# Replacing the framework's scheduler by hand-made semaphores, a TensorE hardware loop and a turned MLP in a decode layer

## The chip, the cores and the metric

The kernel runs on one core of one Trainium2 chip. The metric is the device time of one launch in microseconds (us). All times here are medians of several runs, unless a text says "profiled run", which means the one execution that the hardware profiler recorded. The profiler's span, from the first to the last recorded instruction, is about 1.8 us shorter than the device time of the same run.

Engines are named as the profile names them: PE is TensorE (matmuls), PEld its weight loads, DVE VectorE, ACT ScalarE, POOL GpSimd, SP SyncE. A trailing "q" (SPq, PEq) means the sequencer of that engine. A DMA queue is a list of loads; 16 DMA engines share each bulk load, packet by packet (a tile of 8.39 MB is 128 packets of 64 KB), and the trace records one completion from each of the 16 shares.

## The reference, cut to what matters

It is one decode step of a transformer layer: two batch rows, one token each, 32 heads, and a key and value cache of 8192 positions per head.

```python
# x: (2,1,512)   k_cache, v_cache: (2,32,8192,128) bf16   wq: (512,4096)   wo: (4096,512)
def _A_ref(x, k_cache, v_cache, wq, wo):                 # attention
    q = (x @ wq) -> (2,32,1,128)
    scores = einsum("bhqd,bhkd->bhqk", q, k) * 128**-0.5
    p = softmax(scores)
    o = einsum("bhqk,bhkd->bhqd", p, v)
    return o.reshape(2,1,4096) @ wo
def _B_ref(x, W_gate, W_up, W_down):                     # F = 1376
    gate = x @ W_gate;  gate = gate * (gate > 0)
    return (gate * (x @ W_up)) @ W_down
h  = x + _A_ref(layernorm(x), ...)
h2 = h + _B_ref(layernorm(h), ...)
```

Keys and values are 268 MB of the 281.06 MB that must be read. There are no other large costs by nature: the kernel is a stream of loads with arithmetic beside it.

## The kernel before

Four heads form a "quad", 16 quads in all (8 per batch row). A quad's keys and its values are one tile of 128 x 32768 bf16 (8.39 MB) each. The kernel holds two key tiles and one value tile at a time. Per quad, VectorE multiplies the keys by the query, adds halves in a tree and reduces to scores; ScalarE takes the exponentials into `pm`; TensorE makes the 64 "V products" (128x512 each, spread over four column groups); VectorE sums the four "lanes" of the result; TensorE spreads them. All bulk loads are issued by SyncE into one DMA queue.

```python
# tile pools: kring bufs=2, vring bufs=1, ps_o bufs=2, ... ; the framework sets the semaphores
def lanes_of(o):                                               # 4 VectorE operations of 128x128
    nc.vector.tensor_scalar_mul(osb, o[:, 0:Dh], turn_of[:, 0:1])
    for t in range(1, TG):
        nc.vector.scalar_tensor_tensor(out=osb, in0=o[:, t*Dh:(t+1)*Dh], scalar=turn_of[:, t:t+1],
                                       in1=osb, op0=ALU.mult, op1=ALU.add)
# ... two quads of one row share one result tile o ("paired"), so lanes_of runs 10 times, not 16 ...
for n in range(N - 1):
    scores(n);  load_k(n + 2);  collect();  weighted_v(n);  load_v(n + 1)
# ... weights: output weights first, then the last V in four parts, then gate, up, down ...
nc.sync.dma_start(out=wol, in_=A_wo[LQ * G * Dh:, :].rearrange("(h d) n -> d h n", d=P))  # 1 KB pieces
# ... tail: weights of the MLP as the stationary operand, 88 matmuls of 2 columns ...
for c in range(KC):
    for fc in range(FC):
        nc.tensor.matmul(out=ps[0:w, fc, :], lhsT=lhsT, rhs=hd[:, c, :], ...)
```

The softmax here doesn't subtract the row's maximum and nothing guards it: scores larger than these inputs give would overflow.

Of the kernel before, what the change touches and what calls it, by code (L numbers as in the profile page):

```python
# [12 lines left out]
def _view(t, offset, dims):  # L13
    return bass.AP(tensor=t.tensor, offset=t.offset + offset, ap=[t.ap[0]] + list(dims))


@with_exitstack
def kernel(
# [33 lines left out]
    NM = 2  # L52
    Q = P // G
    ENG = mybir.EngineType

    assert Sq == 1 and Hkv == Hq and D == KC * P and Hq % (2 * G) == 0 and T % 32 == 0 and P == Dh

    consts = ctx.enter_context(tc.tile_pool(name="consts", bufs=1))
    misc = ctx.enter_context(tc.tile_pool(name="misc", bufs=1))
    kring = ctx.enter_context(tc.tile_pool(name="kring", bufs=2))  # L60
    vring = ctx.enter_context(tc.tile_pool(name="vring", bufs=1))
    spool = ctx.enter_context(tc.tile_pool(name="spool", bufs=1))
    opool = ctx.enter_context(tc.tile_pool(name="opool", bufs=1))
    ps_acc = ctx.enter_context(tc.tile_pool(name="ps_acc", bufs=1, space=bass.MemoryType.PSUM))
    ps_mm = ctx.enter_context(tc.tile_pool(name="ps_mm", bufs=2, space=bass.MemoryType.PSUM))
    ps_o = ctx.enter_context(tc.tile_pool(name="ps_o", bufs=2, space=bass.MemoryType.PSUM))
    ps_s = ctx.enter_context(tc.tile_pool(name="ps_s", bufs=1, space=bass.MemoryType.PSUM))

    mean_c = consts.tile([P, 1], f32)
    mean_f = _view(mean_c, 0, [[0, P]])  # L70
    zm = consts.tile([P, B, NQ - 1], f32)
    zl = consts.tile([P, B, G], f32)
    eps_t = consts.tile([P, 1], f32)
# [3 lines left out]
    pm = consts.tile([P, R + NG * W2], bf16)  # L77
    row_of = consts.tile([P, Q], f32)
    nc.vector.memset(eps_t, EPS)
    nc.vector.memset(mean_c, 1.0 / D)  # L80
    nc.vector.memset(zm, 0.0)
    nc.vector.memset(zl, 0.0)
    nc.vector.memset(row_of, 0.0)
    ident = consts.tile([P, P], bf16)
    masks.make_identity(nc, ident)
    zero = consts.tile([P, 1], bf16)
    nc.gpsimd.memset(zero, 0.0)
    nc.gpsimd.memset(pm, 0.0)

    SIZES = (4, 2, 1)  # L90
    FIRST = (0, 4, 6)
    turn_of = consts.tile([P, TG], f32)
    lane_of = consts.tile([P, 2, G], f32)
    head_blk = consts.tile([P, G], f32)
    half_blk = consts.tile([P, 2], f32)
    pick = {n: consts.tile([P, Q // n], f32, name=f"pick{n}") for n in SIZES}
    spread = {n: consts.tile([P, min(n, 2), G, Q // n], f32, name=f"spread{n}") for n in SIZES}
    same = {n: consts.tile([P, n, G, Q // n], f32, name=f"same{n}") for n in SIZES}

    def build_masks():  # L100
        def red(out, in_, axis=AXIS.X):
            nc.vector.tensor_reduce(out=out, in_=in_, axis=axis, op=ALU.add)

        red(turn_of, ident.rearrange("p (g t h) -> p t g h", t=TG, h=G), AXIS.XY)
        red(lane_of, ident.rearrange("p (g u t h) -> p u h g t", u=2, t=TG, h=G), AXIS.XY)
        red(head_blk, ident.rearrange("p (h m) -> p h m", h=G))
        red(half_blk, ident.rearrange("p (u m) -> p u m", u=2))
        red(row_of[:, 0:B], ident.rearrange("p (g q) -> p q g", q=Q)[:, 0:B, :])
        for n in SIZES:
            u = min(n, 2)  # L110
            red(pick[n], ident.rearrange("p (h m) -> p m h", m=Q // n))
            nc.vector.tensor_copy(spread[n], _view(lane_of, 0, [[G, u], [1, G], [0, Q // n]]))
            nc.vector.tensor_copy(same[n], _view(head_blk, 0, [[0, n], [1, G], [0, Q // n]]))

    ctx.enter_context(tc.manual_schedule(engines={ENG.PE, ENG.DVE, ENG.Activation, ENG.SP}))

    warm = consts.tile([1, 1], f32)
    nc.scalar.activation(out=warm, in_=eps_t[0:1, :], func=ACT.Sqrt)


    x_row = opool.tile([B, D], bf16, tag="row")
    nc.scalar.dma_start(out=x_row, in_=A_x.rearrange("b s d -> (b s) d"))
    RING = T * Dh
    wq_sb = vring.tile([P, RING], bf16, tag="v", name="wq_sb")[:, 0:KC * Hq * Dh].rearrange(
        "p (c n) -> p c n", c=KC)
    nc.sync.dma_start(out=wq_sb, in_=A_wq.rearrange("(p c) n -> p c n", p=P))

    def centred(hc, pfx):

        hs = misc.tile([P, B], f32, name=pfx + "hs")  # L130
        nc.vector.tensor_reduce(out=hs, in_=hc.rearrange("p c b -> p b c"), axis=AXIS.X, op=ALU.add)
        mu = ps_s.tile([P, B], f32, tag="st", name=pfx + "mu")
        nc.tensor.matmul(out=mu, lhsT=mean_f, rhs=hs, start=True, stop=True)
        return mu.unsqueeze(1).to_broadcast([P, KC, B])

    def variance(d, pfx):
        sq = misc.tile([P, KC, B], f32, name=pfx + "sq")
        nc.vector.tensor_tensor(out=sq, in0=d, in1=d, op=ALU.mult)
        ss = misc.tile([P, B], f32, name=pfx + "ss")
        nc.vector.tensor_reduce(out=ss, in_=sq.rearrange("p c b -> p b c"), axis=AXIS.X, op=ALU.add)  # L140
        var = ps_s.tile([P, B], f32, tag="st", name=pfx + "var")
        nc.tensor.matmul(out=var, lhsT=mean_f, rhs=ss, start=True, stop=True)
        return var


    x_ps = ps_s.tile([P, KC, B], f32, tag="st")
    x_v = x_row.rearrange("b (m c) -> b m c", c=KC)
    for c in range(KC):
        nc.tensor.matmul(out=x_ps[:, c, :], lhsT=x_v[:, :, c], rhs=ident[0:B, 0:B],  # L149
                         start=True, stop=True)  # L150
    xc = misc.tile([P, KC, B], f32)
    nc.vector.tensor_copy(xc, x_ps)  # L152
    xd = misc.tile([P, KC, B], f32)
    nc.vector.tensor_tensor(out=xd, in0=xc, in1=centred(xc, "ln1"), op=ALU.subtract)
    rstd = misc.tile([P, B], f32)
    nc.scalar.activation(out=rstd, in_=variance(xd, "ln1"), func=ACT.Sqrt, bias=eps_t, scale=1.0)
    nc.vector.reciprocal(out=rstd, in_=rstd)
    xn = misc.tile([P, KC, B], bf16)
    nc.vector.tensor_tensor(out=xn, in0=xd, in1=rstd.unsqueeze(1).to_broadcast([P, KC, B]),
                            op=ALU.mult)  # L160
    xnb = opool.tile([P, KC, B, Q], bf16, tag="row")
    nc.vector.tensor_copy(xnb, xn.unsqueeze(3).to_broadcast([P, KC, B, Q]))
    nc.scalar.activation(out=warm, in_=xn[0:1, 0, 0:1], func=ACT.Exp)
    build_masks()


    qrep = consts.tile([P, B, NQ, Dh], bf16)
    QP = 4
    wq_v = wq_sb.rearrange("p c (i h d) -> p c i h d", h=G, d=Dh)
    for g in range(0, NQ, QP):  # L170
        for h0 in range(0, G, 2):
            qps = ps_mm.tile([P, QP, Dh], f32, tag="mm", name="qps")
            for h in range(2):
                for c in range(KC):
                    nc.tensor.matmul(  # L175
                        out=qps[h * B * Q:(h + 1) * B * Q],
                        lhsT=xnb[:, c].rearrange("p b q -> p (b q)"),
                        rhs=wq_v[:, c, g:g + QP, h0 + h, :],
                        start=(c == 0), stop=(c == KC - 1),
                    )  # L180
            for b in range(B):
                for h in range(2):
                    src = qps[(h * B + b) * Q:(h * B + b + 1) * Q]
                    dst = qrep[(h0 + h) * Q:(h0 + h + 1) * Q, b, g:g + QP, :]
                    if h == 0:
                        nc.scalar.activation(out=dst, in_=src, func=ACT.Copy)  # L186
                    else:
                        nc.vector.tensor_copy(dst, src)  # L188


    seq = [(b, i) for b in range(B) for i in range(NQ)]
    N = len(seq)
    LQ = NQ - 1
    kts, vts = {}, {}

    def load_part(t, cache, n, lo, hi):
        b, i = seq[n]
        src = cache[b, G * i:G * i + G].rearrange("h s d -> (h s) d").rearrange(
            "(p t) d -> p t d", p=P)
        nc.sync.dma_start(out=t[:, lo:hi, :], in_=src[:, lo:hi, :])  # L200

    def load_k(n, cuts=(0, T)):
        kts[n] = kring.tile([P, T, Dh], bf16, tag="k", name="k")
        for lo, hi in zip(cuts[:-1], cuts[1:]):
            load_part(kts[n], A_k_cache, n, lo, hi)
# [83 lines left out]
    def collect():  # L289

        if not pair.get("done"):
            return
# [276 lines left out]
```

## Time and profile before

| What | Value | Where it is read |
|---|---|---|
| time | 661.36 us (661.24 to 661.72, 3 runs) | the runs |
| span of the profiled run | 659.4 us | head of the page |
| DMA queue busy | 98.9% of 16 engines | DMA queue section |
| VectorE busy | 609.6 us, 92% | busy section |
| TensorE busy | 119.5 us, 18% | busy section |
| last packet of the weights | 655.22 us | DMA records of the trace |
| output issued | 656.41 us | timeline of SyncE |
| end of the program | 659.43 us | last record |

The page of the kernel before. The first line gives, by engine, busy time, share and number of instructions; the DMA and GB/s lines are 40 slices of the span; the q lines give packets, MB and share of the 16 DMA engines; the lines with an L are groups of instructions (count, then busy time and mean ns of one, then idle time ahead of them and what ended it).

```profile
PE 119.5 (18%) x1341; PEld 58.6 (9%) x1341; DVE 609.6 (92%) x225; ACT 55.8 (8%) x142; POOL 2.5 (0%) x8
...
DMA  9999999999999999999999999999999999999996
GB/s 382 445 445 445 395 433 446 437 445 418 417 445 437 441 442 398 445 445 426 441 417 433 445 422 441 437 417 441 426 441 441 421 438 426 433 441 433 393 420 259
...
q1 hardware_dynamic: 7272, 281.06, 98.9%
q8 instruction: 10, 0.16, 0.1%
...
L257 PE MATMUL o<-v,pm 128*32 128x512 bf16 x1016 | 88.1, 522 | 395.8 <-DMA v<-in_A_v_cache_dram 395.8
...
L266 DVE TENSOR_SCALAR osb<-o,turn_of 128x128 f32<-128x128 f32 x10 | 3.4, 344 | 9.2 <-PE o L257 9.2
L268 DVE SCALAR_TENSOR_TENSOR osb<-o,turn_of,osb 128x128 f32<-128x128 f32 x30 | 10.5, 351 | 1.1
```

The DMA line is full from the first slice to the last but one. 281.06 MB in the 651 us between the head and the tail are 432 GB/s; the windows view gives 433 GB/s from 2 to 600 us (single slices above read up to 446). In the same trace a packet of 64 KB takes 2.42 us on its share (median of 3840 packets), which is 27.1 GB/s, and 16 such shares are 433 GB/s. So the queue moves what its packets allow, with no gap to close. TensorE waits 395.8 us for V tiles, so whatever is saved on TensorE is saved in idle time.

The slice below 400 GB/s near the end is one of the few things that can move. This is the windows view of the kernel before: the window, its length, busy time with the number of instructions for PE, PEld, DVE, ACT and POOL, TensorE clock, DMA share, GB/s.

```profile
610.00:625.00 15.00, 7.09 (x70) 3.30 (x70) 14.93 (x3) 0.00 (x0) 0.00 (x0) 0.61 0.95 386
```

Here the output weights of the last quad arrive in pieces of 1 KB (a packet of that size took 0.046 us in this trace, 22 GB/s on its share against the 27.1 of a 64 KB packet). The two last lines that matter are the load that starts VectorE's waits in the second half, in the chain of the kernel before (start, length, what), and the issue of the output, in its timeline of SyncE (start, length, what).

```profile
246.27 38.86 DMA k<-in_A_k_cache_dram
```

```profile
656.41 0.65 SPq L537 DMA_DIRECT2D out_dram<-y_row  x1
```

From 246 us on the chain steps through one key load after another, so until then VectorE and afterwards the queue is the one that ended last. VectorE's idle time between its first product of keys (24.49 us) and its last sums (631.86 us) adds up to 14.6 us.

### The profile page before, as it was taken

The page shows a single profiled execution, that of the slowest core. Times are in us where ns is not written, and L with a number is a line of the kernel's source. Part 1 is how long each engine was busy: PE and PEld are TensorE (multiplying, and loading weights), DVE is VectorE, ACT ScalarE, POOL GpSimd, SP SyncE. Part 2 cuts the span into 40 slices and gives each one's busy share as a digit, 9 for nine tenths or more (in the row PEclk, how much of TensorE's full clock was granted, in tenths as well). Part 3 has the DMA queues.
Part 4 walks back from the last instruction along what each step waited for, and adds up shares of the span by engine and source line. Part 5 has one row for each costly group of instructions (what it writes and reads, how often), then busy time and mean ns, then how long its engine had stood idle before and what let it go on. Part 6 is the DMA issues. An engine that isn't in the chain of part 4 may idle for free.

```text
span 659.4 us, 3234 instructions
## 1 busy us (share of the span) xinstructions
PE 119.5 (18%) x1341; PEld 58.6 (9%) x1341; DVE 609.6 (92%) x225; ACT 55.8 (8%) x142; POOL 2.5 (0%) x8
## 2 busy tenths in 40 slices
PE   2100302003030210303012130301202030020446
PEld 1000101001010100101001110100001010010225
DVE  2899999999999999999999999999999998999952
ACT  2201001010101001010101001010010101001020
POOL 1000000000000000000000000000000000000000
PEclk9555755757565575756557575555757555575656
DMA  9999999999999999999999999999999999999996
GB/s 382 445 445 445 395 433 446 437 445 418 417 445 437 441 442 398 445 445 426 441 417 433 445 422 441 437 417 441 426 441 441 421 438 426 433 441 433 393 420 259
DMA packets 7314, 281.26 MB, mean 427 GB/s; under 512 B 802, under 2 KB 1412, under 8 KB 2308
## 3 DMA queue, kind: packets, MB, share of 16 engines
q1 hardware_dynamic: 7272, 281.06, 98.9%
q8 instruction: 10, 0.16, 0.1%
q14 instruction: 4, 0.03, 0.0%
q10 hardware_dynamic: 28, 0.01, 0.0%
HBM read 281.06 MB, written 0.00 MB: 426 GB/s over the span
## 4 chain that ended last, share of the span: by engine, by line
DVE 62%; DMA 33%; PE 3%; issue 1%; ACT 0%; DVEq 0%
DMA k<-in_A_k_cache_dram 31%; DVE k L222 29%; DVE k L228 28%; DVE sc L231 4%; DMA wq_sb<-in_A_wq_dram 2%; DVE osb L268 1%; DVE qrep L188 1%; PE qps L175 1%; PE o L257 1%; PE ar_ps L452 0%; ACT qrep L186 0%; PE y_ps L466 0%; PE a_ps L459 0%; PE gate_ps L510 0%; PE up_ps L510 0%
## 5 line engine op out<-in xcount | busy, mean ns | idle before, releaser
L222 DVE TENSOR_TENSOR k<-k,qrep 128x32768 bf16<-128x32768 bf16 (+1 forms) x17 | 275.7, 16217 | 8.9 <-DMA k<-in_A_k_cache_dram 8.8
L228 DVE TENSOR_TENSOR k<-k 128x16384 bf16<-128x16384 bf16 (+3 forms) x68 | 266.8, 3923 | 2.3
L257 PE MATMUL o<-v,pm 128*32 128x512 bf16 x1016 | 88.1, 522 | 395.8 <-DMA v<-in_A_v_cache_dram 395.8
L234 ACT ACTIVATE pm<-sc 32x256 bf16<-32x256 f32 x64 | 47.2, 738 | 563.9 <-DVE sc L231 527.6
L257 PEld LDWEIGHTS <-pm 128*32 128x32 bf16 x1016 | 37.9, 127 | 444.8 <-issue 282.3
L231 DVE TENSOR_REDUCE sc<-k 128x256 f32<-128x2048 bf16 (+1 forms) x17 | 36.7, 2161 | 1.6
L307 PE MATMUL rep<-osb,spread 128*64 128x128 f32 (+1 forms) x16 | 5.9, 474 | 110.5 <-DVE osb L268 110.5
L234 ACT ACTIVATION_READ_ACCUMULATOR pm<-sc 32x1 f32 x64 | 15.0, 234 | 0.0
L307 PEld LDWEIGHTS rep<-osb,spread 128*64 128x64 f32 (+1 forms) x16 | 3.2, 257 | 114.1 <-DVE osb L268 114.1
L188 DVE CAST qrep<-qps 32x512 bf16<-32x512 f32 x8 | 5.5, 692 | 7.2 <-ACT qrep L186 7.1
L266 DVE TENSOR_SCALAR osb<-o,turn_of 128x128 f32<-128x128 f32 x10 | 3.4, 344 | 9.2 <-PE o L257 9.2
L268 DVE SCALAR_TENSOR_TENSOR osb<-o,turn_of,osb 128x128 f32<-128x128 f32 x30 | 10.5, 351 | 1.1
L175 PE MATMUL qps<-wq_sb,xnb 128*64 128x512 bf16 x32 | 6.5, 562 | 7.0 <-DMA wq_sb<-in_A_wq_dram 4.8
L186 ACT ACTIVATE qrep<-qps 32x512 bf16<-32x512 f32 x8 | 4.7, 586 | 8.5 <-PE qps L175 5.2
L152 DVE COPY xc<-x_ps 128x8 f32<-128x8 f32 x1 | 0.2, 167 | 4.9 <-PE x_ps L149 4.9
L510 PEld LDWEIGHTS <-W 128*128 128x128 bf16 (+1 forms) x88 | 3.8, 126 | 0.3 <-issue 0.3
L175 PEld LDWEIGHTS <-xnb 128*64 128x64 bf16 x32 | 2.7, 147 | 10.0 <-issue 5.3
L452 PE MATMUL ar_ps<-W,oc 128*2 128x512 bf16 x28 | 3.2, 626 | 1.8 <-DVE oc L357 1.8
L297 PE MATMUL o_l<-lane_of,osb 128*128 128x4 f32 x2 | 0.6, 364 | 12.8 <-DVE osb L268 12.8
L317 DVE TENSOR_TENSOR rep<-rep,pick 128x128 f32<-128x128 f32 x6 | 1.8, 295 | 1.0 <-PE rep L307 0.9
L330 PE MATMUL zb<-zm,same 128*128 128x4 f32 (+2 forms) x12 | 2.3, 306 | 0.3 <-DVE ol_f L298 0.3
L330 PEld LDWEIGHTS zb<-zm,same 128*128 128x128 f32 x12 | 2.1, 258 | 0.8 <-issue 0.4
(92 smaller groups left out, 44.3 us busy)
## 6 DMA issues: line engine op xcount, KB each, us to landing
k<-in_A_k_cache_dram SPq DMA_DIRECT2D x2, 4096.0 KB
wq_sb<-in_A_wq_dram SPq DMA_DIRECT2D x1, 4096.0 KB, 12.3
v<-in_A_v_cache_dram SPq DMA_DIRECT2D x1, 4096.0 KB, 13.3
v<-in_A_v_cache_dram SPq DMA_DIRECT2D x1, 3072.0 KB, 20.2
W<-in_A_wo_dram SPq DMA_DIRECT2D x1, 2048.0 KB
W<-in_B_W_gate_dram SPq DMA_DIRECT2D x1, 1376.0 KB
W<-in_B_W_up_dram SPq DMA_DIRECT2D x1, 1032.0 KB, 27.4
W<-in_A_wo_dram SPq DMA_DIRECT2D x1, 1024.0 KB, 29.0
```

Source lines behind the costliest of these rows:

```text
L175: nc.tensor.matmul(out=qps[h * B * Q:(h + 1) * B * Q], lhsT=xnb[:, c].rearrange("p b q -> p (b q)"), rhs=wq_v[:, c, g:g + QP, h0 + h, :], ...
L186: nc.scalar.activation(out=dst, in_=src, func=ACT.Copy)
L188: nc.vector.tensor_copy(dst, src)
L222: nc.vector.tensor_tensor(out=kp, in0=kp, in1=_view(qrep[:, b, i, :], 0, [[0, hi - lo], [1, Dh]]), op=ALU.mult)
L228: nc.vector.tensor_tensor(out=kp[:, :, 0:half], in0=kp[:, :, 0:half], in1=kp[:, :, half:width], op=ALU.add)
L231: nc.vector.tensor_reduce(out=sc[:, lo:hi], in_=kp[:, :, 0:8], axis=AXIS.X, op=ALU.add)
L234: nc.scalar.activation(out=p_of[ps, :, :, h], in_=sc[ps, :].rearrange("p (g t) -> p g t", t=TG), func=ACT.Exp, accum_out=(zm[ps, b, i:i + ...
L257: nc.tensor.matmul(out=o[g:g + W2], lhsT=_view(pm, (0 if lane else R) + t // TG * W2, [[1, W2]]), rhs=vt[:, t:t + TG, :].rearrange("p t d ...
L268: nc.vector.scalar_tensor_tensor(out=osb, in0=o[:, t * Dh:(t + 1) * Dh], scalar=turn_of[:, t:t + 1], in1=osb, op0=ALU.mult, op1=ALU.add)
L307: nc.tensor.matmul(out=reps[where][at:at + m, max(k - 1, 0), :], lhsT=spread[n_of].rearrange("k u h m -> k (u h m)"), rhs=osb, start=True, ...
L330: nc.tensor.matmul(out=zb, lhsT=lhsT, rhs=z, start=True, stop=True)
L510: nc.tensor.matmul(out=ps[0:w, fc, :], lhsT=lhsT, rhs=hd[:, c, :], start=(c == 0 and fc == 0), stop=(c == KC - 1), skip_group_check=True)
```

## The change

The intent: take the framework's scheduler and pools away, order every engine by hand, let TensorE run one short loop instead of a long unrolled program, take small DMA pieces and small matmuls out of the tail, and place the last V products right behind those before. The diff, cut to its core (the whole is a rewrite; cuts are marked by "..."):

```diff
+class Streams:                       # one list of instructions per engine, own semaphores
+    def needs(self, eng, reads, writes, extra): ...     # waits not already known to be over
+    def dma(self, eng, name, fn, ...):                  # one semaphore for each DMA
+        return self.op(eng, fn, reads, writes, extra, (name, 16), (name, 16))
...
-    kring = ctx.enter_context(tc.tile_pool(name="kring", bufs=2))        # and 8 more pools
+    ctx.enter_context(tc.tile_critical(no_gpsimd_drain=True))
+    kt = [sbuf(f"k{s}", (P, T, Dh), bf16) for s in range(2)]
...
+            with nc.Fori(0, NLOOP // NS, engines=OrderedEngineSet([pe.engine]), ...):   # 12 quads
+                with pe.Fori(0, NS):
+                    pe.wait_ge(s.sem("v_in"), 16).then_inc(s.sem("v_in"), -16)
+                    pe.wait_ge(s.sem("p_in"), 1).then_inc(s.sem("p_in"), -1)
+                    pe.wait_ge(s.sem("o_in"), 1).then_inc(s.sem("o_in"), -1)
+                    v_matmuls(o_ps[0], 0, T).then_inc(s.sem("pe"), 1)
+                pe.wait_ge(s.sem("o_in"), 1)
+                for u in range(NS):
+                    last = spread_row(u)
+                last.then_inc(s.sem("pe"), 1)
...
-        nc.vector.tensor_scalar_mul(osb, o[:, 0:Dh], turn_of[:, 0:1])       # lanes: 10 x 4 operations
-        for t in range(1, TG):
-            nc.vector.scalar_tensor_tensor(out=osb, ...)
+        s.op("dve", lambda: dve.tensor_tensor(out=om..., in0=o..., in1=turn..., op=ALU.mult), ...)
+        fn = lambda: dve.tensor_reduce(out=osb[:, u, :], in_=om..., ...)    # lanes: 16 x 2 operations
...
+    weighted_v(L - 1, 0, T // 2)
+    load_v(L, 0, T // 2)                        # the last V right behind its predecessor
+    weighted_v(L - 1, T // 2, T)
+    load_v(L, T // 2, T * 7 // 8)
+    load_v(L, T * 7 // 8, T)
+    for k in range(NGR):
+        load_wo(k)                              # output weights after it, 16 KB pieces
...
+    lanes(L - 1)
+    for lo, hi in zip((0, T // 2, LATE, T * 7 // 8), (T // 2, LATE, T * 7 // 8, T)):
+        weighted_v(L, lo, hi)
...
+    s.op("dve", lambda: dve.transpose(out=ht, in_=ar_ps.rearrange(...)), ...)   # h turned
+                last = pe.matmul(out=ps[j * Q:(j + 1) * Q, :],                  # MLP: 24 x 512 columns
+                                 lhsT=hd[:, c]..., rhs=wgu[:, g, c, offs[j]:offs[j] + MT], ...)
...
+    with nc.Block(no_gpsimd_drain=True) as block:
+        block.sync(lambda e: s.emit("sp", sync))
+        ...
+    for sem in s.sems.values():                 # 45 semaphores, one instruction each
+        pool.sem_clear(sem)
```

## The prediction

> **What bounds the kernel now.** The DMA queue. The page's slices show DMA at 9 tenths in 39 of 40; the DMA section gives one queue 98.9% of 16 engines' span and 281.06 MB. Windows of 5 us show no hole from about 2 us to about 653 us of the 659.4 us span: 281.06 MB in 651 us is 432 GB/s. [...] VectorE is busy 92%: 36.1 us for one quad's scores and 1.4 us for the lanes in the chain of waits, against about 38.8 us of DMA for one quad (16.78 MB). From 246 us on the chain runs through the K loads. TensorE (119.5 us busy) has ample slack. Only three pieces can move: the head before the first packet (2 us), small-packet losses from 610 to 655 us, and the tail from the last weight packet (653.5) to the end.
>
> **What the change does.**
> - TensorE loop over 12 quads: the instruction queues moved 0.19 MB in all, so at most 0.4 us of DMA is saved. Branches hide in the 395.8 us that V products wait for V. One o bank instead of two: the lanes before are done some 18 us before V lands, so no new wait.
> - K and V keep bytes, order and buffers. The queue kept 14 us in reserve (V issued at 581.5, K landed at 595.5); it should not run dry.
> - Last V directly behind V14, output weights after it, in 16 KB instead of 1 KB pieces: windows 610 to 625 fell to 390 to 420 GB/s, worth 0.3 to 1 us.
> - h turned on VectorE, MLP with activations stationary: 24 matmuls of 512 columns packed in threes instead of 88 of 2 columns (3.4 us). Estimated from the V products (64 packed in 6.3 us), 3 to 4 us: no gain. The output weights now land late (643.5 us) and start the tail chain: projection 1.8, turn and mean 2.3, gate and up 3.7, act and its columns 1.6, y rows 1.9 (estimates from the same operations before). That issues the output near 655.3 instead of 656.4.
> - Added: block entries at the start (0.3 us), exits with barriers (one took about 0.3 us after 658.74), and 45 separate semaphore clears on GpSimd after the last barrier, where nothing hides them. The one range clear before took 0.10 us, its successor started after 0.125 us; 45 at 0.06 to 0.12 us are 2.7 to 5.4 us.
>
> **Sum.** Start +0.3, DMA -0.7, tail chain -0.7, exits +0.5, clears +3: about 2 us slower, 663 us. Nearly all that is taken away lies off the critical path; what is added at the end lies on it.
>
> Predicted 663.0 us, 8 in 10 between 657.5 and 667.5. Faster by over 2%: 0.02; within 2%: 0.96; slower: 0.02.
>
> **What would show it.** DMA share still about 99%, 430 GB/s or more up to about 653 us; the chain still through the K loads in the second half; fewer bytes on the instruction queues; the output issued at 654 to 656 us; a train of GpSimd clears of 3 us or more after it landed.
>
> **What would make it wrong.** A hole in the DMA queue where V15 follows V14, or V loads late [...]; clears of 30 ns or less (then about 660 us); a shorter tail chain because packed matmuls run at full clock (granted clock was 0.50 in most of the last windows).

The sum: its five terms come to +2.4 us, entered as about 2 us slower, 663 us. The 0.3 us for block entries is an estimate for which the text gives no source; the trace of after has the first load 0.2 us later.

## The result, and the profile after

| | before | after |
|---|---|---|
| median of 6 runs, same rounds | 661.31 us (661.23 to 661.72) | 663.95 us (663.50 to 665.26) |
| ratio | 1 | 1.0043 (95%: 1.0030 to 1.0056) |

The ratio is the mean time of one kernel's fast runs over that of the other's of the same rounds, so it is not quite the ratio of the medians. The change made the kernel 2.6 us slower, which counts as "within 2%". Predicted were 663.0 us.

The profiled run of the kernel after happens to be the slowest of its six (665.26 us). A later control run of the same file was typical (664.00 us). So lines of both are used below, and each fence says which.

The page of the kernel after, with the lines that answer to those of before:

```profile
PE 118.7 (18%) x1226; PEld 49.5 (7%) x1226; DVE 618.0 (93%) x184; ACT 59.4 (9%) x155; POOL 3.3 (0%) x14
...
GB/s 379 440 443 443 439 387 443 439 443 443 439 415 415 443 439 443 439 439 423 411 443 439 443 439 439 423 411 443 439 443 439 439 424 411 443 429 419 427 426 138
...
q1 hardware_dynamic: 6600, 281.06, 98.2%
q8 instruction: 4, 0.07, 0.0%
...
L406 PE MATMUL o<-v,pm 128*32 128x512 bf16 x1024 | 96.1, 555 | 435.8 <-PEq L430 381.4
...
L450 DVE TENSOR_TENSOR om<-o,turn_of 128x512 f32<-128x512 f32 x16 | 10.9, 682 | 6.8 <-PE o L406 6.8
L454 DVE TENSOR_REDUCE osb<-om 128x128 f32<-128x512 f32 x16 | 16.5, 1028 | 0.6
```

Three things are to be seen. The bytes are the same and the stream is as full, except for the last slice, which fell from 259 to 138 GB/s because the span now has a longer end in which nothing is loaded. The queue of TensorE's instruction fetches (q8) went from 10 packets and 0.16 MB to 4 and 0.07 MB: that is the hardware loop. And the lanes cost VectorE more: 10 x (0.344 + 3 x 0.351) = 14.0 us before, 16 x (0.682 + 1.028) = 27.4 us after.

The windows view of the kernel after, same window and columns as before:

```profile
610.00:625.00 15.00, 3.60 (x32) 1.09 (x32) 14.86 (x6) 1.98 (x7) 0.00 (x0) 0.60 1.00 429
```

The slow stretch is gone: 429 instead of 386 GB/s. The chain of the kernel after, its first step through a key load after the start:

```profile
400.04 40.40 DMA k<-in_A_k_cache_dram
```

It turns to the key loads only from 400 us on, where the chain of before did so from 246 us. That is the mark of the used-up slack: VectorE's idle time between first product and last sums is 6.5 us now, against 14.6 us.

Two lines of the end carry the argument: the issue of the output, in the timeline of SyncE of the profiled run of the kernel after, and the wait of SyncE for GpSimd, in the waits of the engine SP in the same run (waited for, us in total, times, longest).

```profile
656.83 0.66 SPq L723 DMA_DIRECT2D out_dram<-sc  x1
```

```profile
SPq L152 <- POOLq L152: 3.3, 1, 3.3
```

In the control run the output is issued at 655.54 us, that is 0.87 us earlier than before; this is its line in the timeline of SyncE of that run:

```profile
655.54 0.66 SPq L723 DMA_DIRECT2D out_dram<-sc  x1
```

The wait has no counterpart before: at the end of the section that L152 of the kernel opens (`tile_critical`), SyncE waits 3.3 us for GpSimd, which is still clearing semaphores. GpSimd's own records (instructions of its sequencer, not counted as busy; start, length in us) read:

```
after:   659.104 0.048 GpSimd EVENT_SEMAPHORE_RANGE_CLEAR
         659.179 0.044 GpSimd EVENT_SEMAPHORE_RANGE_CLEAR
         659.249 0.044 GpSimd EVENT_SEMAPHORE_RANGE_CLEAR
         ... (45 of them, 0.071 us from start to start, but for one gap of 0.43 us near the end)
         662.515 0.044 GpSimd EVENT_SEMAPHORE_RANGE_CLEAR
         662.586 0.044 GpSimd EVENT_SEMAPHORE_RANGE_CLEAR
before:  659.040 0.096 GpSimd EVENT_SEMAPHORE_RANGE_CLEAR      (the only one)
```

They take 3.5 us after everything else is over. (Two of the expectations below say 44 clears; the trace has 45 of this line, and 90 in the run that clears twice.) So the account of a typical run after (the control) against before is:

| part of the span | before | after | difference |
|---|---|---|---|
| first load issued | 0.74 | 0.95 | +0.2 |
| last packet of the weights | 655.22 | 654.32 | -0.9 (the +0.2 within it) |
| from there to the issue of the output | 1.19 | 1.22 | 0.0 |
| from there to the end | 3.02 | 6.64 | +3.6, of which 3.5 are the clears |
| sum | 659.43 | 662.18 | +2.75 (the control runs measured +2.7: 663.98 against 661.25) |

Three questions were left for the chip. Are the clears really the whole loss (theory), or does the changed tail, where 77 of the 132 matmuls after 641 us started at a granted clock of 0.5 in the profiled run (175 of 260 before), have a part in it (rival)? What made the last packet come 0.9 us earlier? And did the change spend VectorE's slack, as the idle times say, without the time showing it?

### The profile page after: what moved, and what is told of

Read it like the earlier page. It is cut to its first block, busy times and chain, and to the rows that moved or that the text cites. A ratio compares the mean times of both kernels' runs of the same rounds, so it can differ in the third digit from the quotient of the medians.

```text
span 663.5 us, 3097 instructions
## 1 busy us (share of the span) xinstructions
PE 118.7 (18%) x1226; PEld 49.5 (7%) x1226; DVE 618.0 (93%) x184; ACT 59.4 (9%) x155; POOL 3.3 (0%) x14
## 4 chain that ended last, share of the span: by engine, by line
DVE 74%; DMA 22%; PE 3%; issue 1%; SPq 0%; ACT 0%; DVEq 0%
DVE k L363 34%; DVE k L369 33%; DMA k<-in_A_k_cache_dram 22%; DVE sc L226 5%; DVE osb L454 1%; PE o L406 1%; DVE om L450 1%; PE mm L605 1%; PE o L663 0%; PE mm L663 0%; PE y L654 0%; DVE osb L620 0%; DVE qrep L683 0%; PE mm L601 0%; PE st L636 0%
## 5 line engine op out<-in xcount | busy, mean ns | idle before, releaser
L363 DVE TENSOR_TENSOR k<-k,qrep 128x32768 bf16<-128x32768 bf16 (+3 forms) x18 | 275.9, 15327 | 5.0 <-DMA k<-in_A_k_cache_dram 5.0
L369 DVE TENSOR_TENSOR k<-k 128x4096 bf16<-128x4096 bf16 (+6 forms) x72 | 267.4, 3713 | 2.5
L406 PE MATMUL o<-v,pm 128*32 128x512 bf16 x1024 | 96.1, 555 | 435.8 <-PEq L430 381.4
L382 ACT ACTIVATE pm<-sc 32x256 bf16<-32x256 f32 (+2 forms) x68 | 48.2, 709 | 563.0 <-DVE sc L226 562.3
L406 PEld LDWEIGHTS o<-v,pm 128*32 128x32 bf16 x1024 | 40.2, 132 | 490.6 <-issue 478.8
L226 DVE TENSOR_REDUCE sc<-k 128x256 f32<-128x2048 bf16 (+2 forms) x17 | 36.7, 2160 | 0.6
L450 DVE TENSOR_TENSOR om<-o,turn_of 128x512 f32<-128x512 f32 x16 | 10.9, 682 | 6.8 <-PE o L406 6.8
L454 DVE TENSOR_REDUCE osb<-om 128x128 f32<-128x512 f32 x16 | 16.5, 1028 | 0.6
L348 DVE CAST qrep<-mm 32x512 bf16<-32x512 f32 x4 | 2.8, 695 | 10.6 <-PE mm L332 10.6
L332 PE MATMUL mm<-v,om 128*64 128x512 bf16 x32 | 6.5, 570 | 8.2 <-DMA v<-in_A_wq_dram 8.0
L345 ACT ACTIVATE qrep<-mm 32x512 bf16<-32x512 f32 x12 | 7.0, 586 | 8.6 <-PE mm L332 8.4
L332 PEld LDWEIGHTS mm<-v,om 128*64 128x64 bf16 x32 | 2.4, 148 | 11.9 <-issue 9.9
```

The costliest lines, as they stand in the source:

```text
L226: s.op("dve", lambda: dve.tensor_reduce(out=out_, in_=in_, axis=axis, op=ALU.add), reads=reads, writes=writes)
L332: last = pe.matmul(out=ps[h * B * Q:(h + 1) * B * Q], lhsT=xnb[:, c].rearrange("p b q -> p (b q)"), rhs=wq_h[:, c, g:g + QP, h0 + h, :], s ...
L345: s.op("act", lambda src=src, dst=dst: act.activation(out=dst, in_=src, func=ACT.Copy), reads=[f"mm{t}"], writes=[key])
L348: s.op("dve", lambda src=src, dst=dst: dve.tensor_copy(dst, src), reads=[f"mm{t}"], writes=[key])
L363: s.op("dve", lambda: dve.tensor_tensor(out=kp, in0=kp, in1=_view(qrep[:, b, i, :], 0, [[0, hi - lo], [1, Dh]]), op=ALU.mult), reads=keys ...
L369: s.op("dve", lambda half=half, width=width: dve.tensor_tensor(out=kp[:, :, 0:half], in0=kp[:, :, 0:half], in1=kp[:, :, half:width], op=AL ...
```

## The experiments

Every result but those of the two cut V loads is meant to be right, and all passed the comparison with the reference. A first version of the third experiment was never run: `lanes(15)` overwrote `om` while the reduction of `lanes(14)` could still be reading it; a wait was added.

### One clear instead of 45

```diff
-    for sem in s.sems.values():
-        pool.sem_clear(sem)
+    nums = sorted(sem.num for sem in s.sems.values())
+    assert nums == list(range(nums[0], nums[-1] + 1))
+    pool.sem_clear(range(nums[0], nums[-1] + 1))
```

> The 44 single semaphore clears at the end become one range clear over the same 44 semaphores. Theory A (the train of clears is the whole of the slowdown, because nothing runs beside it): in the trace of the changed kernel the clears start 71 ns apart and the train with the one that follows lasts from 659.10 to 662.63 us, so about 3.4 us go and the time falls to about 660.5 us. Rival B (the clears only fill a time that the exit barriers or the runtime need anyway): less than 1 us is gained, 663 us or more. Rival C (the tail chain on TensorE makes it slower): 663 us as well.

Measured: 660.65 us (660.49 to 662.00, 5 runs), ratio 0.9995 to before (0.9982 to 1.0009). The span of the profiled run is 658.9 us, the wait of SyncE for GpSimd is gone from the waits, and the clear of the range of 45 took 0.29 us. Against the median of the kernel after (663.95) that is 3.3 us less. The clears are the loss: one range clear of 0.29 us stands where 45 single ones took 3.5 us. Two of the five runs were 1.1 to 1.3 us above the other three; this is left open here and taken up below.

### Each semaphore cleared twice

```diff
-    for sem in s.sems.values():
+    for sem in list(s.sems.values()) * 2:
         pool.sem_clear(sem)
```

> Each of the 44 semaphores is cleared twice. If each clear costs its 71 ns of start-to-start on the path: 44 times 0.071 is 3.1 us more, about 667.1 us[...]. If they hide: no change.

Measured: 666.97 us (666.78 to 667.15, 4 runs), 3.0 us above the kernel after. The waits of SP in this run hold the same line as above, doubled:

```profile
SPq L152 <- POOLq L152: 6.5, 1, 6.5
```

45 more clears cost 3.0 us of time and 3.2 us of wait: 0.07 us each. Taking away and doubling agree, so the clears are shown to be the cause, with a linear price.

### The last V products ahead of the spread of quad 14

```diff
-    lanes(L - 1)
     for lo, hi in zip((0, T // 2, LATE, T * 7 // 8), (T // 2, LATE, T * 7 // 8, T)):
         weighted_v(L, lo, hi)
+    lanes(L - 1)
```

In the kernel after, TensorE must first do the small spread matmul of quad 14, which waits for VectorE, which is still scoring the last keys. So "the last V directly behind its predecessor" holds for the load, not for the products. Two fences show TensorE's timeline (start, length, what, count, idle time before and who ended it), first of the kernel after (profiled run), then of this experiment:

```profile
634.39 0.42 PE L413 MATMUL rep<-osb,spread 128*32 128x128 f32 x1 [15.99 <-DVE osb L454]
...
634.82 6.26 PE L406 MATMUL o<-v,pm 128*32 128x512 bf16 x61
```

```profile
625.42 3.33 PE L406 MATMUL o<-v,pm 128*32 128x512 bf16 x32 [7.14 <-ACT pm L382]
631.75 1.90 PE L406 MATMUL o<-v,pm 128*32 128x512 bf16 x16 [2.99 <-DMA v<-in_A_v_cache_dram]
634.11 1.55 PE L406 MATMUL o<-v,pm 128*32 128x512 bf16 x16 [0.47 <-ACT pm L382]
```

> Only TensorE's order changes: the 64 products of the last V stand before the small spread matmul of the quad before it, which waits for VectorE until 634.4 us. In the profile of the changed kernel all 64 products ran from 634.5 to 641.1 us although 48 of them had their data by 631.8 us. Theory A (this order costs time in the tail): products 1 to 48 end before 633 us, the last 16 by about 636 us, the rows of attention start near 640 us, and the output is issued about 1 us earlier than in the profile of the changed kernel (656.8), where the last down weights (landed 654.9) hold it; median 0.5 to 1.2 us lower, about 663 us, and the spread between runs (663.5 to 665.3) shrinks. Rival (the last weights hold the tail already, so the order is free): no change within 0.3 us.

Measured: 664.14 us (664.05 to 664.38, 5 runs), ratio 1.0040 (1.0027 to 1.0054). The V products ended at 635.66 us instead of 641.08, more than 5 us earlier, and the time did not move. The output was issued at 655.65 us. What holds the output in a typical run lies behind: it is the last weights, whose last packets landed at 654.47 us, 1.2 us earlier. So the rival was right: in a typical run the order is free. The spread of the runs was 0.3 us, but that says nothing for the new order: the control had 0.5 us with the old one, and the unrolled kernel 0.1 us.

### Both

The edits of the first and the third experiment together: one range clear, and `lanes(L - 1)` behind the last V products. There is no other difference to the kernel after.

> One range clear and the last V's products first. If the two effects lie one behind the other on the same path they add: about 3.4 plus 0.5 to 1.2 us, so 659.4 to 660.1 us, below the 661.3 us of the kernel before. If one hides the other: about 660.5 us.

Measured: 660.99 us (660.65 to 661.31, 5 runs), ratio 0.9994 (0.9980 to 1.0007). The two gains did not add up: 660.5 us was expected for that case, and the single range clear alone had the lower median (660.65). No run of this kernel lay above 661.31. It is not clear of the noise: its median is 0.5 us below that of before in the same rounds (661.51), and the interval holds 1.

### The hardware loop unrolled

```diff
-            with nc.Fori(0, NLOOP // NS, engines=OrderedEngineSet([pe.engine]), head_slot={pe.engine: 0}):
-                with pe.Fori(0, NS):
+            for _ in range(NLOOP // NS):
+                for _ in range(NS):
```

> TensorE's loop over 12 quads is unrolled again by the recording program, waits and all else unchanged. Theory A (the loop is off the critical path; it saved only instruction bytes): within 0.4 us of the changed kernel's 663.95 us; the instruction queues move some 0.1 MB more. Rival (branches and refetching hold up V's products, hence V's loads, hence the stream): 1 us or more faster than the changed kernel.

Measured: 665.24 us (665.17 to 665.27, 5 runs), 1.3 us above the kernel after. Neither theory had foreseen a slower kernel. (The rival's refetching is not in the trace: in the profiled run of the kernel after, TensorE's queue fetched nothing between 27.1 and 542.5 us.) The unrolled kernel fetches as much as the kernel before; this is its page, the line of TensorE's instruction queue:

```profile
q8 instruction: 10, 0.16, 0.1%
```

The last packet of the weights landed at 655.53 us, 1.2 us later than in the control. So the loop is worth 1.2 to 1.3 us although TensorE sits idle for most of the span. Because the loads' order is the same in both, the delivered bytes can be compared at fixed times. This table gives how far the queue was ahead of the kernel before's (in us; the difference of the bytes delivered by then, over 433 GB/s; negative is behind), worked out from the packets of the traces:

| at us | 10 | 300 | 500 | 600 | 625 | 650 | last packet |
|---|---|---|---|---|---|---|---|
| after (control) | -0.2 | +0.1 | +0.4 | +0.4 | +0.9 | +0.9 | +0.9 |
| unrolled | -0.2 | -0.4 | -0.4 | -0.3 | +0.2 | +0.2 | -0.3 |

Three separate effects can be read off. The start is 0.2 us late in both. Between 10 and 500 us the loop gains 0.6 us and the unrolled program loses 0.2; the 0.8 us between them come with the instruction fetches (a later experiment adds fetches alone). Between 610 and 625 us both gain 0.5 us: that fits the bigger pieces of the output weights, though no run changes the pieces alone. The last column adds something to the unrolled program's loss: at 654 us it had delivered as many bytes as before within 0.01 MB, but the last few packets came 0.3 us later. The last packet depends on the slowest of the DMA engines, not on the mean of them.

The sixteen completions of each load show where the 1.2 us arises (they are semaphore increments in the trace's records; no view prints them). Up to 634 us the loads of the unrolled kernel are complete 0.2 us or more before those of the control. The load complete at 639.47 us is still 0.1 us ahead; the next one, at 645.71 us, is 1.2 us behind, and so are all that follow. Between them lies one fetch of TensorE, at 641.89 us. Across it the last completion of a load moved from 1.99 to 3.35 us after the first. Such a fetch of 16,384 bytes had put one share back by 1.55 us in the control too (at 27.8 us: from 0.99 to 2.54); the fetch itself takes about 1.05 us, and in the middle of the unrolled run the 64 KB packet behind it took 2.90 to 2.97 us instead of 2.42. Five more of them by 500 us, spread over 16 engines, are by estimate 0.5 us of mean delay (5 x 1.55 us / 16), a good part of the 0.8 us above; but what ended this run 1.2 us later is, in this one trace, a single fetch near the end that met a share already late. What decides which share a fetch meets is not shown, so neither is it shown that the loop would gain as much elsewhere.

The timeline of TensorE also shows here how the last weights hold the output. The last group of products in the unrolled kernel:

```profile
655.80 0.55 PE L653 MATMUL y<-k,v 128*2 128x128 bf16 x12 [0.23 <-DMA k<-in_B_W_down_dram]
```

It starts when the last of W_down has landed, and the output is issued at 656.72 us. In eight of the nine profiled runs with full loads and no added fetches the output came 1.18 to 1.24 us after the last packet; the exception is the first profiled run of the kernel after.

### Less to load

The time of a kernel that is bound by the queue should fall by what is no longer loaded, until the next limit is met. So of quad 5's values only a sixteenth was loaded, in the kernel after and in the kernel before. The result is wrong (most of the tile still holds the values of the quad before; the comparison's tolerance did not notice). 7.86 MB less are 18.1 us of queue at 433 GB/s.

```diff
 # kernel after
-        fn = lambda: sync.dma_start(out=vt[:, lo:hi, :], in_=rows_of(A_v_cache, n)[:, lo:hi, :])
+        top = T // 16 if n == 5 else hi
+        fn = lambda: sync.dma_start(out=vt[:, lo:top, :], in_=rows_of(A_v_cache, n)[:, lo:top, :])
 # kernel before
+        if n == 5:
+            vts[n], cuts = vts[4], (0, T // 16)
+        else:
+            vts[n] = vring.tile([P, T, Dh], bf16, tag="v", name="v")
```

> Changed kernel, but of the V of quad 5 only a sixteenth is loaded (result wrong on purpose): 7.86 MB less, 18.1 us of the queue at 433 GB/s. Theory A (the DMA queue alone bounds): about 18 us faster, 646 us. Theory B (VectorE is nearly as long: it sat idle only 6.5 us between its first product and its last sums in the changed kernel's trace): at most 6.5 us faster, about 658 us.

> The same cut in the kernel before (result wrong on purpose). Theory A: about 18 us faster, 643 us. Theory B: VectorE sat idle 14.6 us between its first product and its last sums in that kernel, so up to 14.6 us faster, about 647 to 649 us; the difference to the cut in the changed kernel, some 8 us, is the slack that the change's longer lane sums took from VectorE.

Measured: the kernel after fell to 658.22 us (657.12, 657.50, 658.94 and 661.75, an unusually wide set), 5.7 us less. The kernel before fell to 650.79 us (650.17 to 652.17), 10.6 us less. Neither fell by 18.1 us. The kernel before could follow further because it had 14.6 us of idle VectorE time, where the kernel after has 6.5; in the runs with less to load 5.8 (before) and 3.7 us (after) of it were left. The output now came 7.2 and 5.9 us after the last packet (1.2 with full loads), so the arithmetic and no longer the queue ended the run. This confirms in time what the idle times said: the change took slack from VectorE, at no price as long as the loads are as large as they are.

### The kernel after again, as a control

> The changed kernel once more, on the chip of the next two runs: 663.95 us within 0.5 us, in two groups about 1.2 us apart (663.5 to 664.1 and 664.9 to 665.3), as in its first six runs. It is the control for the two below.

Measured: 663.98 us (663.63 to 664.14, 5 runs), ratio 1.0041 (1.0027 to 1.0055), on a third chip. The difference of 2.7 us repeats. All five runs lay together; the upper runs that the first six had (664.89 and 665.26) did not come back.

### Instruction fetches alone

Unrolling may change more than the fetches: TensorE's own records differ too (a V product took 546 ns in the mean, 555 in the kernel after). So here the loop stays, and GpSimd, which has nothing to do in the middle of the kernel, got 2310 instructions of no use: 210 clears of a semaphore that nobody uses, after each of 11 quads. They wait only for products that are long done, and nothing waits for them, but they must be fetched.

```diff
-    for name in ("v_in", "p_in", "o_in"):
+    for name in ("v_in", "p_in", "o_in", "fill"):
         s.sem(name)
 ...
+        if 1 <= n <= 11:
+            s.wait("pool", [v_done(n - 1)])
+            s.lists["pool"].append(((), lambda: [pool.sem_clear(s.sem("fill")) for _ in range(210)] and None, None))
```

> The changed kernel with 2310 idle instructions on GpSimd (clears of an unused semaphore, 210 after each of 11 quads, 71 ns each, so some 15 us of each quad's 38 us on an engine that has nothing else to do). They wait for nothing on the critical path and nothing waits for them; they only have to be fetched[...]. Theory A (each fetch holds up one of the 16 DMA engines, and the last weights land when the slowest engine is done, which is why the unrolled loop cost 1.2 us): last weights land near 655.5 instead of 654.3 us, time 0.8 to 1.5 us above the control's lower group, as the unrolled loop. Rival (unrolling cost time on TensorE, not on the DMA engines): no change beyond 0.3 us.

Measured: 674.70 us (674.21 to 675.22, 5 runs), ratio 1.0203 (1.0189 to 1.0217, so "unclear" at the limit of 2%). That is 10.7 us above the control of the same rounds, where about 1 us was expected: the direction held and the size was missed by a factor of about ten. Its page, the line of the second instruction queue, q14 (4 packets and 0.03 MB in the kernel after; the other 18 are those of GpSimd's 2310 added instructions, about 128 for each packet), and the group of the key products with its wait:

```profile
q14 instruction: 22, 0.18, 0.1%
...
L363 DVE TENSOR_TENSOR k<-k,qrep 128x32768 bf16<-128x32768 bf16 (+3 forms) x18 | 275.9, 15328 | 14.9 <-DMA k<-in_A_k_cache_dram 14.9
```

The same group waited 5.0 us for keys in the kernel after. Eighteen more packets of 8,192 bytes each, 0.15 MB in all, cost 0.3 us if they are counted as bytes at 433 GB/s. They cost 10.7 us because of where they run. The packets of the last key tile in the trace show it: its last four packets (64 KB each) ended at 598.14, 600.55, 602.97 and 605.38 us, 2.42 us apart. 64 KB in 2.42 us are 27 GB/s, a sixteenth of 433 GB/s: one DMA engine working alone, while the other fifteen were done by about 596 us. That engine had fallen behind by about 10 us. The records do not name the engine of a packet, but the sixteen completions of each load show one late share. At the load of 148 us it came 1.90 us after the eighth of the sixteen, at that of 458 us 11.04 us: 9.1 us more over 14 of the added fetches, 0.65 us for each. (Two fetches that the control has as well are not counted.) Of the 64 KB packets that started between 80 and 470 us, 19 took more than 2.6 us, and each of them stands right behind one of the 19 fetches of that stretch (17 added, two of the control's own). The clears, some 15 us of them in each quad, slowed no other packet. So it was the fetches, and not the clears themselves, that held up the loads. The two timelines of VectorE, first of this run, then of the control, show the first product of that tile:

```profile
605.78 12.96 DVE L363 TENSOR_TENSOR k<-k,qrep 128x24576 bf16<-128x24576 bf16 x1 [0.74 <-DMA k<-in_A_k_cache_dram]
```

```profile
595.78 12.96 DVE L363 TENSOR_TENSOR k<-k,qrep 128x24576 bf16<-128x24576 bf16 x1 [0.72 <-DMA k<-in_A_k_cache_dram]
```

Ten microseconds later, and everything behind moved by as much; the queue meanwhile ran nearly empty, as the windows view of this run shows:

```profile
612.00:620.00 8.00, 3.60 (x32) 1.24 (x32) 7.97 (x2) 0.00 (x0) 0.00 (x0) 0.50 0.31 135
```

The packets show what a fetch costs. It starts when a 64 KB packet of the load ends and takes 0.31 to 0.33 us; the 64 KB packet that starts at its end takes 2.77 us instead of 2.42 (2.64 behind the last). That is 0.66 us for each, 11.9 us for 18, and the late share was 11.9 us behind at the load of 516 us, 10.4 at that of 595. Why the packet behind a fetch takes longer is not shown. TensorE's fetches of 16,384 bytes are recorded with 1.02 to 1.14 us each in the profiled runs of before and after. So a fetch takes a turn from the loads: here 0.66 us with the slower packet behind it. Every tile of this kernel comes in 16 shares and is used only when the slowest has landed (fifteen shares of the last key tile were done by about 596 us, the last at 605.38, the first product started at 605.78), so one engine that is behind delays the whole tile.

### TensorE kept busy ahead of the tail

The first profiled run of the kernel after issued its output 2.4 us after the last packet, the others with full loads and no added fetches 1.2. In that run TensorE's granted clock was 0.5 in nearly all of the tail (from 634 to 653.8 us, but for 3.4 us from 640.2 on). Would more work ahead of it raise the clock? These 32 products go into an unused bank, while VectorE is still scoring.

```diff
+    def keep_busy():
+        for _ in range(32):
+            last = pe.matmul(out=mm_ps[1], lhsT=ident, rhs=vt[:, 0:TG, :]..., ...)
+        return last
+    s.op("pe", keep_busy, reads=["va", "ident"], writes=["mm1"])
     lanes(L - 1)
```

> The changed kernel with 32 idle matmuls of 512 columns on TensorE between 624.5 and 634 us, in the time in which it waited for the spread of quad 14. Theory A (the runs of the changed kernel fall in two groups because the 64 products of the last V run from 634.4 us at half clock in some and partly at full clock in others, and only at half clock is the chain on TensorE longer than the last weights): the granted clock is 1.0 when the products start, they take 3.3 to 4.5 us instead of 6.6, and all runs lie in the lower group, 663.4 to 664.1 us. Rival (the two groups come from the DMA stream): two groups as before.

Measured: 664.26 us (663.59 to 664.40, 5 runs), ratio 1.0044 (1.0030 to 1.0058). In the windows view from 634 to 641 us the clock was 0.99 (0.68 in the control, 0.56 in the kernel after), and the V products took 3.62 us, where the same line reads 6.26 us in the profiled run of the kernel after. The timeline of TensorE in this run:

```profile
634.66 3.62 PE L406 MATMUL o<-v,pm 128*32 128x512 bf16 x61
```

The time stayed, slightly above the lower group that was expected (663.4 to 664.1). Since the control had no upper runs, the experiment could not show whether a higher clock removes them. What the traces do show is the chain of that one run: with the clock at half until 640.2 us and again from 643.6 to 653.8 us, the output product of 16 blocks took 3.58 us (1.94 in the control), and the MLP products then followed each other without waiting for their weights. These are the last products of both, first the profiled run of the kernel after, then the control:

```profile
655.67 0.79 PE L654 MATMUL y<-k,v 128*2 128x128 bf16 x44 [0.28 <-ACT v L705]
```

```profile
653.82 1.36 PE L654 MATMUL y<-k,v 128*2 128x128 bf16 x44 [0.28 <-ACT v L705]
```

In the control, 44 products are stretched over 1.36 us, and the last packet of weights landed at 654.32 us, in the middle of them; in the slow run they come after all weights have landed (654.43 us) and take 0.79 us. So in that run the chain of matmuls, not the weights, set the end, 1.3 us later. The profiled runs of before and after record two granted clocks, 1.0 and 0.5, in stretches that are multiples of 3.41 us (3.41 or 6.83 us at 1.0; 30.72 or 34.13 us at 0.5 in most of the span), but for the last one of the kernel after. A V product (128x512) has a median of 634 ns where it starts at 0.5 and of 379 ns where it starts at 1.0. That the varying place of those stretches is what made the upper runs of 664.9 to 665.3 us, and those of the first experiment, is plausible but rests on one profile.

## Why the prediction was right, point by point

- **"What bounds the kernel now. The DMA queue": right.** 433 GB/s in the middle of both, no hole, and nothing that left TensorE's work showed in the time.
- **"45 separate semaphore clears on GpSimd ... 2.7 to 5.4 us", entered as +3: right.** They took 3.5 us; a single range is 3.3 us faster, twice the clears 3.0 us slower.
- **"Start +0.3", "exits +0.5": small estimates, and about right.** The start was 0.2 (first load at 0.95 us instead of 0.74). Without the single clears, the time from issue of the output to the end is 3.47 us against 3.02, and 0.29 us of it is the range clear (0.10 before), so the exits added about 0.3 us.
- **"Issues the output near 655.3 instead of 656.4": right.** 655.54 us in the control, 655.36 to 655.65 in five more. The profiled run with 656.83 us is the exception explained above.
- **"The instruction queues moved 0.19 MB in all, so at most 0.4 us of DMA is saved": mis-sized.** The loop was worth 1.2 to 1.3 us, or 0.7 to 0.8 us in delivered bytes. The prediction counted fetches as bytes spread over 16 engines. A fetch takes its turn on one engine, which one of 16,384 bytes put back by 1.55 us, and a load is over only with its slowest share; the run with 2310 idle instructions made 10.7 us of 0.15 MB that way.
- **Small pieces "worth 0.3 to 1 us": right.** The queue gained 0.5 us between 610 and 625 us. With the loop, counted in bytes, that makes the -0.9 us that the sum had as -0.7.
- **"Tail chain -0.7", "the output weights now land late (643.5 us) and start the tail chain": the term was wrong.** The prediction placed the last packet of the weights at 653.5 us, so that 2.9 us of arithmetic seemed to follow it; the trace of before has it at 655.22. From the last packet to the issue it took 1.2 us in both, a difference of 0. Even V products that ended 5 us earlier changed nothing. The last weights of the MLP hold the output, not the output weights. The number for the output came right because the queue gained a little more than was assumed, in place of the tail.
- **"The lanes before are done some 18 us before V lands, so no new wait": true, but the lanes' own cost was missed.** The prediction costed "1.4 us for the lanes" of a quad before. It did not say that they now run 16 times instead of 10 at 1.71 us, 13.4 us more in all. Other work on VectorE fell (184 instructions instead of 225), so its busy time rose by 8.4 us (609.6 to 618.0) and its idle time fell from 14.6 to 6.5 us: it fitted. "The chain still through the K loads in the second half" was right only from 400 us on for the same reason. Nothing in its own list of what could go wrong would have warned of more.

The sum was near the truth (663.0 against 663.95) with two of its gains placed wrongly: the loop had too little, the tail too much. The two errors had opposite signs, so part of the closeness is luck; the clears, the largest term, were not.

## What to carry to other kernels

Where one queue is full for 99% of the span, as here, expect little from work taken off other engines; look at the head, at the tail, and at what runs after the last result, where each of the 45 single clears cost its 0.071 us: clear semaphores as one range (3.3 us here). A program that is never waited for can still cost time by being fetched (10.7 us in the run with 2310 idle instructions), because a fetch takes a turn from the loads on a DMA engine (0.66 us for 8,192 bytes there); so a hardware loop can pay even on an engine that idles (1.3 us here, through the engine on which one late fetch fell). And before adding work to an engine that is "not the bottleneck", count its idle time in the bound stretch: this change spent 8 of VectorE's 14.6 us, which showed in the time only in an experiment with less to load.

What stays open: why single runs of the kernel after and of the one with the range clear lie 1 us higher, and whether the order of the last V products would prevent it.
